# Linear attention and ELU feed-forward on one core: 1/P in PSUM, a late check of alpha, and a new issue order

## The chip, the cores and the metric

The kernel runs on one core of a Trainium2 chip. The metric is the device time of one execution in microseconds (us). TensorE is called PE, VectorE DVE, ScalarE ACT, GpSimd POOL and SyncE SP; SP issues nearly all DMAs.

## The reference

```python
B, H, S, D = 4, 8, 768, 48          # attention; then 3072 tokens, d_model 384, d_ff 2048
for t in range(S):
    state = alpha[:, :, t, :, None] * state + np.einsum('bhd,bhe->bhde', k[:, :, t], v[:, :, t])
    y[:, :, t] = np.einsum('bhd,bhde->bhe', q[:, :, t], state)
x = np.ascontiguousarray(y.transpose(0, 2, 1, 3)).reshape(B * S, H * D)
h = x @ w_in
g = np.where(h > 0.0, h, np.exp(np.minimum(h, 0.0)) - 1.0)
out = g @ w_out                      # everything in float32
```

## The kernel before

The attention works in 24 windows of 128 time steps (6 to a batch element), the feed-forward in 12 blocks of 256 tokens (two windows each), with d_ff cut into 8 slices j. Everything is a list of tokens of the form NAME.i: a function NAME is called with the index i and issues one or a few instructions. The list START (L49 to L76) is written out by hand and covers windows 0 to 11 in part and blocks 0 to 3; the list STEADY (L79), from block 4 on, repeats and is not touched. The tokens are issued in exactly this order, so that it sets the order on each engine's queue and on SP's DMA queue. Each engine takes its own instructions strictly in order.

A window i passes through these tokens. L (or LA for alpha and LB for k and q) loads k, q and alpha (`qka`, 770 KB, three buffers); LV loads v (four buffers, which hold the state too). SC (DVE, L202) is the running product P of alpha. LN and EX (ACT, L211, L216) make R = 1/P by a logarithm and an exponential; EX also adds up R into `chk_p`. KA (L224), KB (L229) and KC (DVE, L234) turn k into k/P with one Newton step, on DVE for the windows in KAV and KBV and on POOL for the others. PC (ACT, L238) adds up P into `chk_p`, as a check of alpha's range. SQ (L251, L254) is q times P, on DVE for the windows in SQV, else on POOL. TP (PE, L275) and KN (ACT, L305), or TA and TB (DVE, L285), transpose k. S (PE, L340, L324) and MK (DVE, L357, L352) are the masked scores, U (PE, L387, L369) is k times v, and UP, UA, UB, UC (L413, L404, L406, L435, L437) bring the state forward. YL, Y3 and Y (PE and ACT, L448, L453, L481, L493) make the output of the window, XH, XP, XL and XD split it into a high and a low float32r part.

Weights come in sixteen packed loads F.f (768 KB each; f = 2j for w_in, 2j+1 for w_out). Two of them make a pair p: KW (ACT, L572), DA (DVE, L586) and DB (DVE, L591) unpack a pair, WH (ACT, L618) rounds to the high part, WL (L638, on DVE for the f in WLV, else on POOL) subtracts to the low part. F.13 and F.15 land in a buffer (`spare`) that is read until WL.9 and WL.11 are done. LC, CA and CB check the packed weights later, through the one buffer with the tag `ck`. The feed-forward of block b and slice j is A (PE, 18 matmuls, L654) into a PSUM tile h, RA, RB (ACT), RC (DVE), GH (ACT) and GL (DVE, or POOL for the pairs in GQS; L662 to L693) for the ELU and its split into two parts, and O (PE, 12 matmuls, L707) into two PSUM tiles per block, which stay until Z.b copies them out.

All PSUM tiles come from one pool, `psa`, with 8 banks: a PE token that needs a new tile waits until the last reader of an old one has finished. X and the WARM loop (L126) are fillers, matmuls of 512 columns on constants whose result nobody reads.

Of the kernel before, what the change touches and what calls it, by code (L numbers as in the profile page):

```python
# [973 lines left out]
```

## Time and profile before

| what | value |
|---|---|
| timed runs | 473.01, 475.49, 475.50 us (median 475.49) |
| the profiled execution: its time, and the span of its instructions | 474.23 us, 472.5 us |
| PE busy | 461.9 us (98%) |
| DVE busy | 369.4 us (78%) |
| ACT busy | 313.8 us (66%) |
| POOL busy | 130.6 us (28%) |
| bytes moved by DMA | 61.13 MB, a mean of 129 GB/s |

The page gives busy time for each engine over the span. An engine that waits inside a group of matmuls can still look busy, so the share alone does not say what bounds a stretch; for that one reads the waits (who waited for whom), the timeline of one engine, and the chain of work that ended last. PE is busy in all of the span's 40 slices at 80% or more, apart from the last, and the DMA engines are full in the first five slices and below half after them.

### The profile page before, as it was taken

How to read it: one execution, taken by the hardware profiler on the slowest of the kernel's cores; microseconds unless marked ns; L12 is line 12 of the kernel's file. 1: busy time of each engine (PE TensorE's matmuls, PEld its weight loads, DVE VectorE, ACT ScalarE, POOL GpSimd, SP SyncE). 2: the span in 40 equal slices, each digit the busy share in tenths (PEclk: the TensorE clock that was granted, in tenths of full speed). 3: DMA queues.
4: the chain of work that ended last, by engine and by line, in shares of the span. 5: the costliest groups of instructions: out<-in, count | busy, mean ns of one | idle time of the engine just before them, and what ended most of it. 6: DMA issues, size and time to landing. Idle time of an engine off the chain costs nothing.

```text
span 472.5 us, 13139 instructions
## 1 busy us (share of the span) xinstructions
PE 461.9 (98%) x5413; PEld 446.1 (94%) x5414; DVE 369.4 (78%) x764; ACT 313.8 (66%) x664; POOL 130.6 (28%) x113
## 2 busy tenths in 40 slices
...
GB/s 308 400 411 416 140 1 181 54 104 151 73 115 101 35 173 168 148 73 177 139 72 153 164 68 152 164 72 153 154 84 151 81 88 52 68 44 10 2 35 40
DMA packets 20483, 61.13 MB, mean 129 GB/s; under 512 B 2880, under 2 KB 7872, under 8 KB 20416
## 3 DMA queue, kind: packets, MB, share of 16 engines
...
## 4 chain that ended last, share of the span: by engine, by line
PE 86%; DVE 6%; ACT 3%; DMA 3%; issue 1%; SPq 0%; DVEq 0%; ACTq 0%
PE h L654 37%; PE o L707 36%; PE y L453 4%; PE q L369 2%; PE q L324 2%; DMA raw<-in_wgt_dram 2%; PE wp L126 2%; DVE spare L591 1%; PE y L448 1%; DVE raw L586 1%; DMA qka<-in_qka_dram 1%; DVE w L638 1%; PE sc L340 1%; ACT w L618 1%; PE tp L275 1%
## 5 line engine op out<-in xcount | busy, mean ns | idle before, releaser
L654 PE MATMUL h<-xt,w 128*128 128x256 f32 x1728 | 202.3, 276 | 3.9 <-DVE gl L693 1.5
L654 PEld LDWEIGHTS h<-xt,w 128*128 128x128 f32 x1728 | 197.9, 192 | 5.3 <-DVE gl L693 1.7
L707 PE MATMUL o<-w,gh 128*128 128x384 f32 x768 | 189.0, 328 | 0.0
L707 PEld LDWEIGHTS o<-w,gh 128*128 128x128 f32 x768 | 132.4, 189 | 0.9
L707 PE MATMUL o<-w,gl 128*128 128x384 f32 x384 | 125.4, 327 | 0.0
L662 ACT ACTIVATE r<-h 128x512 f32<-128x512 f32 x96 | 56.5, 599 | 56.6 <-PE h L654 55.2
L285 DVE STREAM_TRANSPOSE kn<-qka 32x128 f32<-32x128 f32 x256 | 77.4, 302 | 4.0
L673 DVE SCALAR_TENSOR_TENSOR h<-r,h 128x512 f32<-128x512 f32 x79 | 53.7, 691 | 25.4 <-ACT r L667 25.0
L707 PEld LDWEIGHTS o<-w,gl 128*128 128x128 f32 x384 | 72.6, 189 | 0.2 <-DVE gl L693 0.2
L693 DVE TENSOR_TENSOR gl<-h,gh 128x512 fp32r<-128x512 f32 x79 | 54.0, 689 | 23.7 <-ACT gh L679 20.7
L679 ACT CAST gh<-h 128x512 fp32r<-128x512 f32 x79 | 46.0, 582 | 34.3 <-DVE h L673 23.4
L224 POOL TENSOR_TENSOR qka<-qka,R 128x512 f32<-128x512 f32 x19 | 25.8, 1360 | 144.1 <-ACT R L216 96.0
L667 ACT ACTIVATE r<-r 128x512 f32<-128x512 f32 x96 | 60.7, 634 | 1.7
L254 POOL TENSOR_TENSOR st<-qka,P 64x512 f32<-64x512 f32 x32 | 40.0, 1249 | 23.1 <-DVE P L202 9.6
L352 DVE TENSOR_TENSOR st<-q,mask 64x256 f32<-64x256 f32 x72 | 30.3, 421 | 8.3 <-PE q L324 7.1
L693 POOL TENSOR_TENSOR gl<-r,gh 128x512 fp32r<-128x512 f32 x17 | 23.7, 1397 | 42.3 <-ACT gh L679 27.9
L202 DVE TENSOR_TENSOR_SCAN P<-qka,first 128x516 f32<-128x516 f32 x24 | 30.8, 1286 | 4.5 <-ACT R L238 2.6
L211 ACT ACTIVATE R<-P 128x512 f32<-128x512 f32 x24 | 15.0, 631 | 28.4 <-DVE P L202 28.3
L604 ACT ACTIVATE ck<-ck,lim 128x384 int32<-128x384 int8 x32 | 23.8, 744 | 3.5 <-DMA ck<-in_wgt_dram 3.5
L609 ACT ACTIVATE ck<-ck,lim 128x384 f32<-128x384 int32 x32 | 23.0, 719 | 0.8
L453 PEld LDWEIGHTS y<-st,vs 128*64 128x64 f32 x576 | 17.7, 138 | 2.4 <-issue 2.3
L229 POOL TENSOR_TENSOR R<-P,R 128x512 f32<-128x512 f32 x16 | 19.0, 1190 | 1.2
...
## 6 DMA issues: line engine op xcount, KB each, us to landing
...
```

The source lines that it names most:

```text
L202: nc.vector.tensor_tensor_scan(out=P.rearrange("p n w -> p (n w)"), data0=t[:, 2 * NP * W:], data1=first.rearrange("p n w -> p (n w)"), in ...
L254: eng(SQV, i).tensor_tensor(out=st[r, a], in0=d["q"][r], in1=pw(i)[r], op=ALU.mult)
L285: nc.vector.transpose(out=kn[32 * t:32 * t + 32, :, 32 * g:32 * g + 32], in_=d["kt"][32 * g:32 * g + 32, :, 32 * t:32 * t + 32])
L352: nc.vector.tensor_tensor(out=d["st"][r, a, :, c * C:(c + 1) * C], in0=d["s4"][a][o], in1=mask[o].unsqueeze(1).broadcast_to([64, NP, C]), ...
L453: nc.tensor.matmul(out[64 * a:64 * a + m], lhsT=lhs(i, c, a)[:, n * D:n * D + m], rhs=d["st"][:, a, n, c * C:(c + 1) * C], start=start, st ...
L654: nc.tensor.matmul(h[:, f, :], lhsT=t[:, wi, ws], rhs=x[:, :, c, xi].rearrange("p a x -> p x a"), start=(f == 0 and k == 0), stop=(k == 8) ...
L662: nc.scalar.activation(out=r, in_=d["h"], func=AF.Relu, scale=-1.0)
L667: nc.scalar.activation(out=d["r"], in_=d["r"], func=AF.Exp, scale=-1.0)
L673: nc.vector.scalar_tensor_tensor(out=d["g"], in0=d["r"], scalar=-1.0, in1=d["h"], op0=ALU.add, op1=ALU.max)
L679: nc.scalar.copy(out=gh, in_=d["g"])
L693: q.tensor_tensor(out=gl, in0=d["g"], in1=d["gh"].bitcast(F32), op=ALU.subtract)
L707: nc.tensor.matmul(o[:, 0:DM], lhsT=gt[:, f, ms], rhs=t[:, wi, f * DM:f * DM + DM].rearrange("p (a x) -> p x a", a=2), start=(j == 0 and f ...
```

## The change

Window by window, R of windows 0 to 4 (RPS) is now a tile of the PSUM pool; POOL can't read PSUM, so KA and KB of these windows are all on DVE, and the lists KAV, KBV, SQV and WLV change. The sum over P of windows 0 to 5 (ALATE; PC) is gone. In its place LP loads alpha of that window a second time, into the buffer with the tag `ck`, and AC (ACT) makes one pass over it, relu(2^100 (alpha - 1.25)), with its sum into the same place of `chk_p`. WARM is 20, not 25. The matmuls of YL and Y of windows 0 to 5 go in another order: the two halves a of the partitions now alternate. START has the same tokens otherwise, in a new order; X.2.0 no longer stands first, and X.2.2 has gone ahead of TP.0. The diff, cut (of START the first lines of both; two more tuples, WHV and KNV, are empty and choose nothing):

```diff
 EARLY = 6
-WARM = 25
+WARM = 20
 
 
 QU, QS = 2, 6
 
 PAIRS = 10
 
-WLV, KAV, KBV, SQV = (0, 2, 4, 5, 8, 9, 11, 14), (0, 1, 2, 6, 9), (0, 1, 2, 3, 4, 6, 8, 9), (0, 1, 3, 4, 6, 11)
-
-
+WLV, KAV, KBV, SQV = (1, 4, 7, 8, 9, 10, 11, 12, 14), (0, 1, 2, 3, 4, 7), (0, 1, 2, 3, 4, 6, 11), (0, 2, 5, 11)
+
+
+WHV, KNV = (), ()
+RPS, ALATE = (0, 1, 2, 3, 4), (0, 1, 2, 3, 4, 5)
 WPE, XPE, GPE, UPE = (), (0, 1, 2), (), (1,)
...
 START = """
-X.2.0 LA.0 SC.0 LN.0 LB.0 LA.1 SQ.0 EX.0 KA.0 SC.1 KB.0 LB.1 LV.1 LN.1 LV.0 KC.0 TP.0 EX.1 KA.1 KB.1 KC.1 S.0 L.2 SQ.1
-KN.0 F.0 U.0 UC.0 PC.0 TP.1 KN.1 SC.2 LN.2 S.1 MK.1 MK.0 U.1 F.2 SQ.2 EX.2 KA.2 UA.0 L.3 UP.1 UC.1 KB.2 PC.1 YL.0 Y3.0
-DA.0 X.2.2 Y.0 KC.2 TP.2 LV.2 UA.1 YL.1 F.4 SC.3 S.2 KW.0 DB.0 F.6 XH.0 KN.2 LV.4 Y3.1 U.2 UA.2 Y.1 F.1 LN.3 EX.3 MK.2
-YL.2 UB.2 WH.2 WL.2 KA.3 KB.3 XH.1 F.3 Y3.2 F.5 SQ.3 XP.0 XL.0 WH.0 WL.0 XP.1 XL.1 KW.2 KW.1 Y.2 XH.2 DA.2 KC.3 A.0.1
-DB.2 WH.4 TP.3 KN.3 DA.1 WL.4 DB.1 A.0.0 RA.0.0 RB.0.0 LV.3 WH.6 RA.0.1 F.14 WL.6 S.3 U.3 WH.1 A.0.2 WL.1 UC.2 XP.2
-XL.2 MK.3 RA.0.2 UA.3 YL.3 RB.0.1 RC.0.0 F.7 GH.0.0 Y3.3 RB.0.2 WH.3 A.0.3 DA.3 F.8 KW.3 F.10 GL.0.0 WL.3 DA.4 RC.0.1
-Y.3 XH.3 L.4 RC.0.2 UB.3 O.0.0 RA.0.3 GH.0.1 GH.0.2 PC.2 XL.3 DB.3 A.1.3 L.6 A.1.0 F.12 GL.0.2 F.9 KW.4 WH.5 A.1.1
-WH.7 SC.4 LN.4 WL.5 GL.0.1 DB.4 RB.0.3 EX.4 O.0.1 DA.6 A.1.2 WH.10 WL.10 SQ.4 KA.4 LC.2 RA.1.0 RC.0.3 RA.1.3 RB.1.0
-GH.0.3 RC.1.0 F.11 GL.0.3 LV.5 RA.1.1 RB.1.1 DA.5 RB.1.3 RC.1.1 GH.1.0 KW.5 A.1.5 RC.1.3 UC.3 RA.1.5 GL.1.0 WL.7 KB.4
-O.0.2 O.0.3 PC.3 L.5 SC.5 RA.1.2 RB.1.2 GH.1.3 GL.1.3 WH.8 WL.8 RB.1.5 RC.1.5 GH.1.1 RC.1.2 O.1.0 LN.5 KW.6 A.0.4
-RA.0.4 DB.5 LV.7 WH.11 EX.5 RB.0.4 SQ.5 GH.1.2 KC.4 PC.4 DB.6 GL.1.1 RC.0.4 O.1.1 TP.4 KN.4 A.1.4 RA.1.4 GL.1.2 WH.14
-U.4 UA.4 UB.4 RB.1.4 KA.5 KB.5 KC.5 PC.5 RC.1.4 S.4 O.1.2 A.0.5 WH.9 WL.14 UC.4 WL.11 TP.5 KN.5 L.7 GH.0.4 O.1.3 WH.12
-RA.0.5 RB.0.5 WL.9 SC.7 SC.6 GH.1.4 GL.1.4 LN.7 A.1.7 F.13 GL.0.4 WL.12 O.0.4 MK.4 LN.6 RC.0.5 EX.6 U.5 KA.6 Y.4 CA.2
-CB.2 F.15 DA.7 UA.5 SQ.6 RA.1.7 S.5 GH.0.5 GL.0.5 EX.7 LV.6 A.0.6 RB.1.7 MK.5 KW.7 KB.6 KC.6 PC.6 RA.0.6 RB.0.6 A.1.6
-DB.7 O.1.4 GH.1.5 GL.1.5 XH.4 XL.4 RA.1.6 RC.1.7 O.0.5 RC.0.6 RB.1.6 RC.1.6 GH.1.6 TP.6 O.1.5 GL.1.6 S.6 KN.6 WH.13
-KA.7 KB.7 MK.6 Y.5 XH.5 XD.4 WL.13 XL.5 L.9 KC.7 TB.7 WH.15 U.6 GH.1.7 O.1.6 ZV.6 XD.5 WL.15 GH.0.6 GL.0.6 PC.7 L.8
-GL.1.7 SQ.7 A.0.7 RA.0.7 UA.6 UB.6 UC.6 RB.0.7 A.2.1 RA.2.1 O.0.6 RB.2.1 SC.8 LN.8 LC.1 EX.8 KA.8 RC.2.1 GH.2.1 O.1.7
...
+LA.0 LB.0 LA.1 SC.0 LN.0 X.2.2 EX.0 LB.1 L.2 SQ.0 X.2.0 SC.1 LN.1 EX.1 SQ.1 KA.0 KB.0 KC.0 TP.0 KA.1 KB.1 KC.1 LV.0
+KN.0 S.0 LP.3 AC.3 F.0 LV.1 U.0 MK.0 UA.0 F.2 UC.0 TP.1 KN.1 YL.0 Y3.0 SC.2 LN.2 EX.2 LV.2 L.3 F.4 S.1 Y.0 MK.1 XH.0
+SQ.2 KA.2 KB.2 KC.2 DA.0 U.1 UP.1 KW.0 TP.2 KN.2 S.2 UA.1 F.6 U.2 YL.1 UC.1 MK.2 Y3.1 XP.0 UA.2 YL.2 Y3.2 SC.3 LV.3
+DB.0 F.7 Y.1 LN.3 EX.3 KA.3 SQ.3 KB.3 F.5 XL.0 XH.1 WH.2 WL.2 KC.3 WH.0 Y.2 XH.2 LV.5 WL.0 XP.1 XL.1 TP.3 XP.2 S.3
+KN.3 UB.2 U.3 KW.2 DA.2 XL.2 LV.6 MK.3 UC.2 UA.3 A.0.1 KW.3 DB.2 DA.3 WH.4 YL.3 Y3.3 L.4 SC.4 RA.0.1 RB.0.1 A.0.0
+RA.0.0 Y.3 F.1 WH.6 RB.0.0 WL.4 WL.6 XH.3 LN.4 F.3 DB.3 XL.3 EX.4 RC.0.0 A.0.2 RA.0.2 RB.0.2 KA.4 A.1.1 RC.0.1 GH.0.1
+A.1.2 WH.5 F.8 DA.1 RC.0.2 KW.1 L.5 KB.4 KC.4 DB.1 A.0.3 GL.0.1 TP.4 WH.7 GH.0.2 A.1.0 GL.0.2 LP.5 UB.3 RA.1.1 UC.3
+GH.0.0 F.9 KN.4 WH.1 WH.3 GL.0.0 F.10 WL.1 SQ.4 S.4 MK.4 LV.4 U.4 RA.1.0 WL.5 RB.1.0 UA.4 RC.1.0 O.0.0 WL.3 KW.4 SC.5
+DA.4 DB.4 AC.5 A.1.3 RA.1.2 O.0.1 GH.1.0 UB.4 RB.1.2 RB.1.1 RC.1.1 WH.10 RA.0.3 RB.0.3 O.0.2 F.11 L.6 UC.4 GH.1.1
+GL.1.1 WL.10 WH.8 KW.5 RC.0.3 GH.0.3 A.1.5 GL.1.0 RC.1.2 O.1.0 O.1.1 RA.1.5 WL.7 RA.1.3 RB.1.3 GH.1.2 WL.8 DA.5 GL.0.3
+F.14 LN.5 EX.5 F.12 SC.6 DB.5 RB.1.5 LN.6 KA.5 EX.6 A.1.4 RA.1.4 RB.1.4 RC.1.5 O.0.3 L.7 RC.1.3 GH.1.3 WH.11 RC.1.4
+GH.1.4 WH.9 KW.6 A.0.4 RA.0.4 RB.0.4 GL.1.3 GL.1.2 O.1.2 O.1.3 SQ.5 KA.6 KB.6 GH.1.5 KB.5 A.0.5 KC.5 TP.5 GL.1.4 LP.4
+AC.4 RA.0.5 RB.0.5 KC.6 SC.7 TP.6 KN.5 WL.11 RC.0.4 GH.0.4 GL.0.4 WL.9 O.1.4 KN.6 F.15 DA.6 U.6 LN.7 UA.6 Y.4 RC.0.5
+U.5 DB.6 GL.1.5 UB.6 UC.6 LV.7 WH.14 F.13 S.5 L.8 WL.14 A.1.7 UA.5 WH.12 WL.12 KW.7 DA.7 MK.5 A.1.6 RA.1.7 SQ.7 RB.1.7
+RC.1.7 O.1.5 SQ.6 EX.7 RA.1.6 GH.0.5 RB.1.6 RC.1.6 GH.1.6 KA.7 LC.3 A.0.7 XH.4 XL.4 RA.0.7 RB.0.7 RC.0.7 PC.6 O.0.4
+GL.1.6 KB.7 Y.5 XH.5 S.6 DB.7 WH.13 WH.15 A.0.6 GL.0.5 O.0.5 GH.1.7 XD.4 XL.5 KC.7 TB.7 SC.8 WL.13 XD.5 CA.3 CB.3 PC.7
...
     chk_y = const.tile([128, 2, NWIN], F32, name="chk_y")
     nc.vector.memset(chk_y[:, 1, 0:DIRECT], 0.0)
-    lim = const.tile([128, 2], F32, name="lim")
+    lim = const.tile([128, 3], F32, name="lim")
+    nc.vector.memset(lim[:, 2:3], -1.25 * 2.0 ** 100)
     nc.vector.memset(lim[:, 0:1], 0.5625)
     nc.vector.memset(lim[:, 1:2], -9.0)
     win = [{} for _ in range(NWIN)]
+    ck = {}
     TOK = dict(X=X)
...
     @tok
     def LN(i):
-        R = win[i]["R"] = work.tile([128, NP, W], F32, name="R", tag="R")
+        if i in RPS:
+            R = psa.tile([128, NP, W], F32, name="rp", tag="pa")
+        else:
+            R = work.tile([128, NP, W], F32, name="R", tag="R")
+        win[i]["R"] = R
         nc.scalar.activation(out=R, in_=pw(i), func=AF.Ln)
     @tok
...
     @tok
     def PC(i):
         nc.scalar.activation(out=win[i]["R"], in_=pw(i), func=AF.Copy, accum_out=chk_p[:, 1, i:i + 1])
+
+    @tok
+    def LP(i):
+        t = ck["p", i] = work.tile([128, DM, 2], F32, name="cp", tag="ck", bufs=1)
+        nc.sync.dma_start(out=t.rearrange("p k two -> p (k two)")[:, 0:NP * AW], in_=qka[i, :, 2 * NP * W:QW])
+
+    @tok
+    def AC(i):
+        t = ck.pop(("p", i)).rearrange("p k two -> p (k two)")[:, 0:NP * AW]
+        nc.scalar.activation(out=t, in_=t, func=AF.Relu, scale=2.0 ** 100, bias=lim[:, 2:3],
+                             accum_out=chk_p[:, 1, i:i + 1])
     @tok
     def SQ(i):
...
...
     xt = {}
-    def ymm(i, out, n, c, a, m, start):
-        d = win[i]
-        if i < EARLY:
-
-            for s, r in ((0, slice(64 * a, 64 * a + D)), (1, slice(64 * a, 64 * a + 64))):
-                if s or i % NW or c:
-                    nc.tensor.matmul(out[64 * a:64 * a + m], lhsT=lhs(i, c, s)[r, n * D:n * D + m],
-                                     rhs=d["st"][r, s, n, c * C:(c + 1) * C], start=start, stop=True,
-                                     skip_group_check=True)
-                    start = False
+    def ymm(i, out, n, c, m, start):
+        d = win[i]
+        if i >= EARLY:
+            for a in range(2):
+                nc.tensor.matmul(out[64 * a:64 * a + m], lhsT=lhs(i, c, a)[:, n * D:n * D + m],
+                                 rhs=d["st"][:, a, n, c * C:(c + 1) * C],
+                                 start=start, stop=True, skip_group_check=True)
             return
-        nc.tensor.matmul(out[64 * a:64 * a + m], lhsT=lhs(i, c, a)[:, n * D:n * D + m],
-                         rhs=d["st"][:, a, n, c * C:(c + 1) * C],
-                         start=start, stop=True, skip_group_check=True)
+
+        for s in range(0 if i % NW or c else 1, 2):
+            for a in range(2):
+                r = slice(64 * a, 64 * a + (64 if s else D))
+                nc.tensor.matmul(out[64 * a:64 * a + m], lhsT=lhs(i, c, s)[r, n * D:n * D + m],
+                                 rhs=d["st"][r, s, n, c * C:(c + 1) * C], start=start, stop=True,
+                                 skip_group_check=True)
+            start = False
     def xs(i):
         blk, half = divmod(i, 2)
...
             return
         yl = d["yl"] = psa.tile([128, W], F32, name="yl", tag="pa")
         for c in range(2):
-            for a in range(2):
-                ymm(i, yl[:, c * C:(c + 1) * C], NP - 1, c, a, 64, c == 0)
+            ymm(i, yl[:, c * C:(c + 1) * C], NP - 1, c, 64, c == 0)
     @tok
     def Y3(i):
...
                                      start=(n == 0), stop=True, skip_group_check=True)
         for c in range(2):
             for n in range(nn):
-                for a in range(2):
-                    ymm(i, y[:, n, c * C:(c + 1) * C], n, c, a, D if direct else 64,
-                        not direct and c == 0 and n == 0)
+                ymm(i, y[:, n, c * C:(c + 1) * C], n, c, D if direct else 64, not direct and c == 0 and n == 0)
     @tok
     def XH(i):
...
```

## Rows read from the trace of the kernel before

**Rows 1.** The page's busy table: engine, us, share of the span, instructions
```profile
PE 461.9 (98%) x5413; PEld 446.1 (94%) x5414; DVE 369.4 (78%) x764; ACT 313.8 (66%) x664; POOL 130.6 (28%) x113
```

**Rows 2.** Busy time by stretch: length, engines with instructions, clock, DMA share, GB/s
```profile
40.00:50.00 10.00, 10.00 (x125) 9.80 (x124) 9.32 (x11) 9.83 (x16) 4.57 (x2) 1.00 1.02 412
...
165.00:440.00 275.00, 275.00 (x3207) 270.44 (x3206) 225.34 (x526) 185.45 (x416) 65.19 (x56) 1.00 0.36 112
```

**Rows 3.** Waits of PE: engine, tile, line, what ended them; total us, times, longest
```profile
PE h L654 <- DVE gl L693: 1.5, 1, 1.5
PE h L654 <- DVE vs L435: 1.0, 1, 1.0
PE h L654 <- DVE vs L406: 1.0, 1, 1.0
PE h L654 <- DVE kn L285: 0.3, 1, 0.3
PE q L369 <- ACT kn L305: 0.3, 1, 0.3
```

**Rows 4.** Timeline of PE, 2 to 11 us: start, duration, instruction, shape, count
```profile
2.08 8.11 PE L126 MATMUL wp<-first 128*128 128x512 bf16 x25 [2.08 <-DVE first L120]
10.03 0.59 PE L126 MATMUL xf<-first 128*128 128x512 bf16 x2
10.46 0.60 PE L275 MATMUL tp<-ident,qka 128*128 128x128 f32 x4
```

**Rows 5.** Timeline of DVE: GL.0.3, then WL.14, then WL.11 and WL.9
```profile
55.64 0.69 DVE L693 TENSOR_TENSOR gl<-h,gh 128x512 fp32r<-128x512 f32 x1
...
74.09 0.95 DVE L638 TENSOR_TENSOR w<-wm,w 128x768 fp32r<-128x768 f32 x1
...
75.23 1.82 DVE L638 TENSOR_TENSOR w<-spare,w 128x768 fp32r<-128x768 f32 x2
```

**Rows 6.** The chain that ended last: start us, us, what; weights F.13 and F.15
```profile
77.49 8.20 DMA raw<-in_wgt_dram
```

**Rows 7.** The same chain: S.2 and Y.3 on PE
```profile
21.23 0.88 PE sc L340 x31
...
41.32 1.40 PE y L448 x48
```

**Rows 8.** Timeline of DVE, 6 to 10 us: KA.0 and KC.0
```profile
6.40 0.69 DVE L224 TENSOR_TENSOR qka<-qka,R 128x512 f32<-128x512 f32 x1 [0.58 <-ACT R L216]
...
8.85 0.69 DVE L234 SCALAR_TENSOR_TENSOR qka<-R,qka 128x512 f32<-128x512 f32 x1
```

**Rows 9.** Timelines of POOL (WL.10, KA.4) and DVE (SQ.4, two RC), 51 to 56 us
```profile
51.91 1.92 POOL L638 TENSOR_TENSOR w<-spare,w 128x768 fp32r<-128x768 f32 x1 [4.75 <-DMA vs<-in_vv_dram]
53.79 1.72 POOL L224 TENSOR_TENSOR qka<-qka,R 128x512 f32<-128x512 f32 x1
...
52.08 2.30 DVE L251 TENSOR_TENSOR st<-qka,P 128x512 f32<-128x512 f32 x1
54.30 1.28 DVE L673 SCALAR_TENSOR_TENSOR h<-r,h 128x512 f32<-128x512 f32 x2
```

**Rows 10.** PE timeline (A.1.4, A.1.7), then the chain (A.0.6 with A.1.6, two O)
```profile
68.80 2.25 PE L654 MATMUL h<-xt,w 128*128 128x256 f32 x18
...
79.44 2.17 PE L654 MATMUL h<-xt,w 128*128 128x256 f32 x18
...
88.00 4.26 PE h L654 x36
92.25 3.90 PE o L707 x24
```

**Rows 11.** DVE's groups, 0 to 77 us: count, busy us, mean ns (DA, SC, UC)
```profile
L586 DVE TENSOR_SCALAR raw<-raw 128x1536 int32<-128x1536 int32 x7 | 8.9, 1267 | 0.0
L202 DVE TENSOR_TENSOR_SCAN P<-qka,first 128x516 f32<-128x516 f32 x6 | 7.9, 1318 | 1.0 <-DMA qka<-in_qka_dram 0.9
...
L435 DVE TENSOR_TENSOR vs<-q,P 128x192 f32<-128x192 f32 x3 | 1.1, 363 | 0.0
```

31 lines of the change are left out of this document (19 added, 12 removed).

## Prediction

> **What bounds the kernel now.** I read the busy table first [rows 1]: TensorE (PE) is busy 461.9 of 472.5 us, VectorE (DVE) 78%, ScalarE (ACT) 66%. A busy PE need not be a full one, so the stretches came next: from 165 to 440 us PE is busy for all 275.00 us, while from 40 to 50 us DVE and ACT are nearly full too (9.32 and 9.83 of 10) and the DMA engines move 412 GB/s [rows 2]. So the late two thirds are PE work end to end, nothing in them is touched by the diff, and the sum can only be made in the hand-ordered START part: its PE instructions, and the gaps between them. PE's own waits are five there besides the first one: 1.5, 1.0, 1.0, 0.3 and 0.3 us, 4.1 in all [rows 3]. The other thing on PE that computes nothing is the fillers, 25 from 2.08 us and two more from 10.03 us, up to the first real instruction at 10.46 us, TP.0 [rows 4].
>
> The three long waits are all for a PSUM bank (pool `psa`, 8 banks), and each ended with a reader of another tile: A.0.2 with UC.2 (L435), A.1.5 with GL.0.3 (L693), A.0.6 with UA.5 (L406) [rows 3]. UC.2 even stands behind A.0.2 in START. Behind these readers stood DVE: GL.0.3 ended at 56.33 us after DVE passes without a gap; UA.5 stood behind DA.7, which waited for a weight load from 77.49 to 85.69 us [rows 5, 6].
>
> **The change, part by part.** Durations are of the profiled execution: span 472.5 us, 474.23 us with what lies around it. The three timed runs are 473.01, 475.49 and 475.50; the four have a mean of 474.56, and I put the difference on that, as one execution is no better than another.
>
> *Fillers.* Two fillers of X.2.0 take 10.46 - 10.03 = 0.43 us, so 0.216 us each (512 columns, the 2.4 GHz level). The 25 take 7.95 us, which is about 12 at twice that (1.2 GHz) and 13 at 0.216 [rows 4]. The change puts 20 + 2 + 2 = 24 ahead of TP.0 in place of 27: those removed are of the fast kind, 3 x 0.216 = 0.65 us, and TP.0 can start at 9.81. X.2.2 leaves the place between YL.0 and Y.0 (another 0.43 us), where it covered the wait for Y3.0; S.1 (32 matmuls, about 0.9 us by 31 of S.2 in 0.88 us [rows 7]) now stands there and is longer. Total -1.1 us. The cover: TP.0 needs KC.0, which ended at 8.85 + 0.69 = 9.54 us; before KA.0 DVE idled 0.58 us for ACT [rows 8], and the new order puts SC.1 into that gap, so KC.0 ends some 0.5 us earlier, about 9.0. If SC.1's alpha lands late, KA.0 behind it on DVE waits too; ends 0 and +0.3 us, I take 0. Of the clock the rows show that PE ran at the low level for its first 5 us and then at the high one. The page "TensorE: Matmul & The Clock Gate" of the Trainium skill (part 1) says that the moment of the rise differs between runs; with all fillers at the low level three fewer would save 1.3 us in place of 0.65. No run here shows that.
>
> *1/P in PSUM, and KA/KB of windows 3 and 4 on DVE.* An operand in PSUM does not make a DVE pass shorter: KC.0, all in SBUF, took 0.69 us, and two RC passes that read h from PSUM took 1.28 together [rows 8, 9]. What it changes is the neighbourhood of GpSimd (POOL). SQ.4 on DVE, with two SBUF inputs, took 2.30 us beside POOL's WL.10, against the 0.69 of such passes alone; the RC pair, beside POOL's KA.4, was not stretched [rows 9]. So KA and KB of windows 0 to 4 can't be stretched any more, SQ.4 goes to POOL (-1.6 us of stretch on DVE), and KA.4 (1.72 us on POOL [rows 9]) becomes 0.6 us on DVE. The price is a bank from LN to KC.
>
> *PC to LP and AC.* Six ACT passes become six of the same length; three of them (0, 1, 2) move from the full stretch to behind 95 us. Each AC waits on ACT's queue for its own load, with KN, LN and RA behind it: AC.3 is the only one close to its load, and KN.1 behind it has to wait for TP.1 anyway, which stands behind S.0 and U.0. Each LP is 128 x 516 words, 258 KB, 0.64 us at 412 GB/s [rows 2]; only LP.3 and LP.5 go on SP's queue while the DMA engines are full, so F, LV and L loads behind them come 0.64 to 1.3 us later. DVE waited for no weight load before 85 us, so I take 0; ends 0 and +0.6.
>
> *Matmuls of YL and Y.* Old order: 48 in 1.40 us, 29.2 ns each; S, which already alternates the halves, 31 in 0.88 us, 28.4 ns each [rows 7]. 384 matmuls x 0.8 ns: 0 to -0.3 us; I take 0.
>
> *The new order.* All five waits lose their cause as they stand: -4.1 us. What is late next? START's PE work is the same, so I put the time at which PE comes to a piece (old start, corrected for the pieces moved past it, old waits and the 1.1 us) against its last producer on DVE (old end, corrected in the same way). Prices: A 2.13 and O 1.95 us; S 1.0, Y 1.9, TP and U 0.5 (by the two rows of 32 and 48 small matmuls); on DVE 0.6 for a 512-column pass (two RC in 1.28), WL 0.91, SC 1.3, DA 1.27, a U step 0.3 [rows 5, 9, 10, 11].
> - A.1.4 waits for GL.0.3's bank. PE: 68.80 [rows 10] - O.0.3 - A.0.4 (4.1) + S.4 + U.4 (1.5) - 2.5 - 1.1 = 62.6. DVE: GL.0.3 at 56.33 [rows 5], less SQ.1, 3, 4, WL.0, 2, 5, DA.6 and the stretch (7.4), plus 19 pieces moved ahead of it (SQ.2, KA.3, KA.4, KB.4, KC.4, four U steps, WL.1, 7, 8, 10, MK.4, SC.5, RC.1.1, GL.1.0, RC.1.2, DA.5: 12.8): 61.7. Covered by 0.9.
> - A.1.7 waits for WL.14. PE: 79.44 + TP.6, O.1.4, U.6, Y.4, U.5, S.5 (6.4) - 2.8 - 1.1 = 81.9. DVE: WL.14 at 75.04, less 6.2 (the same without DA.6), plus 14.4 (KA.3, 4, SQ.2, 5, WL.1, 7, 9, 10, 11, MK.4, UC.4, SC.6, 7, KB.6, KC.6, GL.1.4, RC.0.5, UB.6, UC.6): 83.2, late by 1.3 if DVE waits as long as before, by nothing if it doesn't.
> - A.1.6, the second of the two from 88.00 us, started at 90.1 [rows 10]; with TP.6, O.1.4, U.6 (3.0) ahead of it and O.0.4, A.0.6 (4.1) not, it comes at 90.1 + 3.0 - 4.1 - 3.8 - 1.1 = 84.1, and may get the bank that MK.5 reads. MK.5 stands behind DA.7, DA.7 waits for F.15 and F.13, which SP sends after WL.9 has freed their buffer. WL.9 ended at 77.05; new order and less stretch leave it there (nine pieces and the stretch go, 10.2; thirteen come, 10.0), less what DVE no longer waits: 73 to 77. The load takes 8.6 us as before (77.05 to 85.69), DA.7 and MK.5 1.9: 83.5 to 87.5, so 0 to 3.4 us late.
>
> New waits thus lie between 0 and some 3.5 us; I take 1.5, the middle of the last one, since the first two are near their cover. Sum: -1.1 - 4.1 + 1.5 = -3.7 us, 470.5 on the profiled execution, **470.9** on the mean of the four.
>
> **Rivals.**
> *All cover holds* (A.1.6 gets another bank, UA.5's): -5.2 us, 469.4. For it: DVE waits less when PE is earlier. Against: the one order that the trace shows has three bank waits.
> *The banks cost as much as before.* Counting the tiles alive in START, the old order has 8 places at which seven banks are taken and the next tile must have the last one; the new has 13, for R stands in a bank and O.1's two follow O.0's sooner. The three bank waits, 3.5 us [rows 3], over 8 places are 0.44 us each, over 13 they are 5.7: 474.56 - 5.2 + 5.7 = 475.1. For it: the waits were of this kind. Against: at A.1.4, one of the 13, cover was found above. Beside it stands the page "PSUM — Partial Sum Buffer" of the Trainium skill (summary: rules for kernel authors), which tells authors to evacuate PSUM promptly as it is tight; keeping R there goes against it, and this rival is what it would do.
> *POOL collides with DVE* (slower). POOL takes WL.0, 2, 3, 5, 6 and SQ.1, 3, 4 ahead of WL.9, beside DVE's two-input DB and SC; each collision costs about the 1.6 us of SQ.4 [rows 9] and puts off WL.9, so the loads of F.15 and F.13, so DA.7, at which both ACT (KW.7) and DVE then stand. A lag of 5.2 + 2.4 us at A.1.6 means WL.9 at about 81.2, three collisions more than now; five more: 474.56 - 5.2 + (8.0 + 3.4) = 480.8. Against: the old order had as many POOL passes there.
> *R in PSUM does nothing*: DVE then keeps its lost time, and the case is that of the banks.
>
> **How the numbers follow.** Forecast 0.48 (469.5 to 472.8); all covered 0.17; banks 0.20; collisions 0.08; 0.07 for what no row shows. The range takes in the two neighbours, with 1.2 us of the runs' own spread below the lower: 468.2 to 475.3. About 0.5% (2.4 us) is what a measurement of this kernel can tell from no change: faster 0.66 (forecast, all covered and a little of the rest), the same 0.25 (banks, some rest), slower 0.09.
>
> **What would show it.** Right: TP.0 at 9.8 us, right behind the fillers; no wait before Y.0; PE's waits within START at 1 to 2 us, the longest near A.1.6 and ended by MK.5 or DA.7; DVE's passes on R at 0.69 us beside a busy POOL. Wrong: PE idle between the fillers and TP.0; new waits of 4 us and more ended by readers of h tiles (banks); DB or SC at 2.5 us and more beside WL on POOL; a wait for LP on ACT with PE behind it; more than 0.2 us of gaps behind 165 us.

## The result: 0.7% slower, where 3.7 us less were forecast

| | before | after |
|---|---|---|
| time, median of 20 runs each | 473.14 us | 477.20 us |
| ratio, 95% interval | | 1.0069 [1.0046, 1.0092] |
| profiled execution: time, span | 474.23, 472.5 us | 478.38, 476.7 us |
| last matmul of PE ends at | 468.44 us | 470.81 us |
| PE idle from its first filler to its last matmul | 4.5 us | 7.0 us |

The range of the forecast ended at 475.3. The medians are of all runs; the ratios here and below compare only runs in the chip's faster state, which leaves out 1 of the 20 of after, 1 of the 6 of tuned and 3 of the 12 of r_sbuf, its profiled one among them, whose idle time isn't given for that reason. In the two profiled executions PE ends 2.4 us later; the other 1.8 us of the span lie behind PE. There the last output takes 3.5 us to land in place of 1.9. It takes 3.8 in before_lpac_psum below, which has the old order, and 1.9 in l4_early, which has the new one, so I don't put that part down to the change.

The page's busy table of after (answers [rows 1]) shows PE as busy as before, in a longer span:

```profile
PE 461.8 (97%) x5409; PEld 446.5 (94%) x5409; DVE 371.3 (78%) x763; ACT 316.6 (66%) x664; POOL 135.1 (28%) x115
```

The waits of PE in after (engine, tile, line, what ended them; total us, times, longest; answers [rows 3]):

```profile
PE h L679 <- DVE w L663: 1.7, 1, 1.7
PE o L732 <- DVE w L663: 1.7, 1, 1.7
PE y L477 <- issue: 1.1, 1, 1.1
PE sc L363 <- DVE gl L718: 0.9, 1, 0.9
PE tp L294 <- POOL st L270: 0.5, 1, 0.5
PE h L679 <- ACT ck L631: 0.4, 1, 0.4
PE u L436 <- issue: 0.3, 1, 0.3
PE h L679 <- DVE vs L458: 0.2, 1, 0.2
```

Not one of the five waits of [rows 3] is left, as forecast. But eight others stand there, 6.8 us in all, and the two longest are not waits for a bank. They are for `w L663`, the low half of a weight (WL), which A.0.2 and O.0.0 read. The timeline of PE has them in their places (start us, duration, instruction, shape, count, idle time before):

```profile
39.20 8.47 PE L679 MATMUL h<-xt,w 128*128 128x256 f32 x70 [1.67 <-DVE w L663]
...
51.01 1.09 PE L363 MATMUL sc<-st,qka 48*64 48x64 f32 x30 [0.89 <-DVE gl L718]
...
54.64 0.43 PE L732 MATMUL o<-w,gh 128*128 128x384 f32 x1 [1.67 <-DVE w L663]
...
57.10 3.24 PE L679 MATMUL h<-xt,w 128*128 128x256 f32 x18
```

The last of these rows is slow for another reason: the same 18 matmuls take 2.17 us elsewhere. PE goes on at 54.64, after the pauses of 0.89 and 1.67 us, and from about 56 us the granted clock falls, to 0.50 of 2.4 GHz (1.2 GHz) up to 59 us and to 0.66 as a mean of these 5 us. It didn't fall behind A.0.2's pause, which was as long, 1.67 us, so the length of a pause alone doesn't decide it (busy time by stretch: length, PE with instructions, granted clock, DMA share, GB/s):

```profile
39.00:44.00 5.00, 4.67 (x39) 1.00 1.03 413
...
50.00:55.00 5.00, 2.44 (x69) 1.00 1.01 386
55.00:60.00 5.00, 5.00 (x28) 0.66 0.43 153
...
56.00:59.00 3.00, 3.00 (x14) 0.50 0.43 144
```

That is (1 - 0.66) x 5 = 1.7 us of matmuls lost, beside the waits themselves.

What DVE did ahead of the three pauses (its timeline: SC.4, WL.4, DB.1, GL.0.2, WL.1):

```profile
35.50 1.23 DVE L206 TENSOR_TENSOR_SCAN P<-qka,first 128x516 f32<-128x516 f32 x1 [1.59 <-DMA qka<-in_qka_dram]
36.65 2.50 DVE L663 TENSOR_TENSOR w<-spare,w 128x768 fp32r<-128x768 f32 x1
...
46.61 3.66 DVE L613 SCALAR_TENSOR_TENSOR spare<-raw 128x1536 int32<-128x1536 int32 x1 [0.35 <-ACT raw L594]
50.15 0.71 DVE L718 TENSOR_TENSOR gl<-h,gh 128x512 fp32r<-128x512 f32 x1
...
52.04 2.54 DVE L663 TENSOR_TENSOR w<-spare,w 128x768 fp32r<-128x768 f32 x1
```

And what POOL did at the same moments (WL.6, WL.5, WL.3):

```profile
36.38 1.95 POOL L663 TENSOR_TENSOR w<-spare,w 128x768 fp32r<-128x768 f32 x1 [5.95 <-ACT w L643]
...
46.59 1.83 POOL L663 TENSOR_TENSOR w<-wm,w 128x768 fp32r<-128x768 f32 x1
51.94 1.82 POOL L663 TENSOR_TENSOR w<-spare,w 128x768 fp32r<-128x768 f32 x1 [3.52 <-ACT w L643]
```

Lay the two side by side. POOL's WL.6 ends at 38.33; DVE's WL.4, which by its row began at 36.65, ends at 39.15, 0.82 us later, about as long as a WL takes alone (0.95 in [rows 5]). POOL's WL.5 ends at 48.42 and DVE's DB.1 at 50.27, 1.85 later, a DB's own time. POOL's WL.3 ends at 53.76 and DVE's WL.1 at 54.58, 0.82 later. Each time POOL began first, by 0.02 to 0.27 us, and the pass on DVE ends as if it had only begun when POOL had finished. The Trainium skill has a rule that says so, on the page "SBUF — State Buffer", section "SBUF: two separate sides": the two engines share one pair of ports, a DVE pass with two SBUF inputs needs it, and whoever comes second waits for the whole instruction of the other. The three pairs of rows agree with it to 0.13 us.

### The profile page after: what moved, and what is told of

It reads as the page before. It is cut to its first block, busy times and chain, and to the rows that moved or that the text cites. A ratio compares the mean times of both kernels' runs of the same rounds, so it can differ in the third digit from the quotient of the medians.

```text
span 476.7 us, 13154 instructions
## 1 busy us (share of the span) xinstructions
PE 461.8 (97%) x5409; PEld 446.5 (94%) x5409; DVE 371.3 (78%) x763; ACT 316.6 (66%) x664; POOL 135.1 (28%) x115
## 4 chain that ended last, share of the span: by engine, by line
PE 79%; DVE 6%; DMA 5%; ACT 4%; issue 2%; SPq 1%; POOL 1%; ACTq 0%; POOLq 0%; DVEq 0%
PE o L732 36%; PE h L679 34%; PE y L469 4%; DMA qka<-in_qka_dram 4%; PE q L347 2%; PE q L392 2%; DMA raw<-in_wgt_dram 1%; DVE w L663 1%; DVE spare L613 1%; DVE gl L718 1%; ACT w L643 1%; PE sc L363 1%; DVE h L698 1%; PE y L477 1%; ACT raw L594 1%
## 5 line engine op out<-in xcount | busy, mean ns | idle before, releaser
L232 POOL TENSOR_TENSOR qka<-qka,R 128x512 f32<-128x512 f32 x18 | 23.7, 1319 | 139.6 <-ACT R L224 89.1
L273 POOL TENSOR_TENSOR st<-qka,P 64x512 f32<-64x512 f32 x34 | 44.8, 1317 | 23.8 <-DVE P L206 9.7
L206 DVE TENSOR_TENSOR_SCAN P<-qka,first 128x516 f32<-128x516 f32 x24 | 29.6, 1233 | 5.7 <-DMA qka<-in_qka_dram 5.6
L219 ACT ACTIVATE R<-P 128x512 f32<-128x512 f32 x19 | 12.0, 629 | 25.4 <-DVE P L206 25.4
L631 ACT ACTIVATE ck<-ck,lim 128x384 f32<-128x384 int32 x32 | 22.9, 717 | 0.8
L237 POOL TENSOR_TENSOR R<-P,R 128x512 f32<-128x512 f32 x17 | 20.2, 1189 | 3.5 <-DVE qka L232 2.3
L469 PEld LDWEIGHTS y<-st,vs 128*64 128x64 f32 x576 | 17.8, 138 | 2.5 <-issue 2.5
```

The source lines that it names most:

```text
L206: nc.vector.tensor_tensor_scan(out=P.rearrange("p n w -> p (n w)"), data0=t[:, 2 * NP * W:], data1=first.rearrange("p n w -> p (n w)"), in ...
L273: eng(SQV, i).tensor_tensor(out=st[r, a], in0=d["q"][r], in1=pw(i)[r], op=ALU.mult)
L469: nc.tensor.matmul(out[64 * a:64 * a + m], lhsT=lhs(i, c, a)[:, n * D:n * D + m], rhs=d["st"][:, a, n, c * C:(c + 1) * C], start=start, st ...
```

## The experiments

Five theories were set against each other. **1**: DVE and POOL exclude each other where DVE reads SBUF alone, and that makes WL.4, DB.1 and WL.1 late. **2**: the late load L.4 holds DVE's queue at SC.4 (1.59 us above), and all else follows from it. **3**: the banks that R takes. **4**, for the wait `y <- issue`, which nothing in the trace releases: PE waits for its own code. And, as in the prediction, each part of the change was to have its own price. In the expectations the pass at 46.61 is called DB.4, and the one that S.4 waits for GL.0.0; by the order on DVE they are DB.1 and GL.0.2.

| kernel | median us | ratio to before, 95% interval | PE idle, us |
|---|---|---|---|
| changed kernel | 477.20 | 1.0069 [1.0046, 1.0092] | 7.0 |
| wl_apart | 474.33 | 1.0027 [0.9998, 1.0055] | 6.3 |
| l4_early | 476.73 | 1.0063 [1.0036, 1.0090] | 5.6 |
| both | 475.62 | 1.0049 [1.0022, 1.0076] | 6.8 |
| r_sbuf | 478.09 | 1.0083 [1.0051, 1.0116] | not given |
| tuned | 476.47 | 1.0079 [1.0050, 1.0107] | 5.6 |
| no_early_lp | 484.93 | 1.0269 [1.0248, 1.0290] | 11.6 |
| f57_late | 480.50 | 1.0141 [1.0110, 1.0172] | 8.0 |
| f4567_late | 480.66 | one run; before 471.66 | 9.5 |
| before_lpac | 485.76 | 1.0275 [1.0254, 1.0296] | 10.6 |
| before_lpac_psum | 489.70 | 1.0360 [1.0339, 1.0380] | 12.6 |
| before_warm20 | 472.63 | 0.9991 [0.9962, 1.0021] | 3.6 |
| before_sq4 | 472.92 | 0.9990 [0.9968, 1.0012] | 3.5 |
| before_best | 470.77 | 0.9937 [0.9913, 0.9962] | 0.8 |

### wl_apart: POOL's three passes put on DVE

```diff
-WLV = (1, 4, 7, 8, 9, 10, 11, 12, 14)
+WLV = (1, 3, 4, 5, 6, 7, 8, 9, 10, 11, 12, 14)
```

> The changed kernel with the low halves WL.3, WL.5 and WL.6 put on DVE instead of POOL; order and all else as changed. In the changed kernel's trace WL.4 (DVE 36.65, 2.50 us), DB.4 (46.61, 3.66 us) and WL.1 (52.04, 2.54 us) each end one lone duration (0.9, 1.8 and 0.9 us) after a pass of POOL that began earlier. Theory 1 (the two engines exclude each other): the three passes take 0.93 to 1.0 and 1.8 us again, the PE waits for A.0.2 (1.67), S.4 (0.89) and O.0.0 (1.67) fall to 0 to 0.5 each, PE doesn't pause long enough to drop to 1.2 GHz behind O.0.0 (2.2 us), while DVE has 3 passes of 0.95 more: 3.5 to 6 us under the changed kernel, 0.994 to 0.999 of before. Theory 2 (the load L.4 comes late and holds the DVE queue from SC.4 on): DVE is as late and has 2.9 us more to do, O.0.0's wait stays at 1.5 or more: 1.004 to 1.010. Theory 3 (banks: the tiles of R take PSUM): the waits stay, 1.007.

Timeline of DVE in wl_apart: WL.4 and WL.6, then DB.1, then WL.1:

```profile
37.16 1.80 DVE L663 TENSOR_TENSOR w<-spare,w 128x768 fp32r<-128x768 f32 x2
...
46.49 1.97 DVE L613 SCALAR_TENSOR_TENSOR spare<-raw 128x1536 int32<-128x1536 int32 x1 [0.41 <-ACT raw L594]
...
50.24 0.95 DVE L663 TENSOR_TENSOR w<-spare,w 128x768 fp32r<-128x768 f32 x1
```

The passes are back at 0.9 each, 1.97 and 0.95 us: theory 1 has the mechanism. O.0.0 and S.4 no longer wait, A.0.2 waits 0.49, and the clock stays at 2.4 GHz. The time falls by 1.0069 - 1.0027 = 0.42%, 2.0 us, where theory 1 had 3.5 to 6; the two intervals just overlap, so that even these 2.0 are not clear of noise. The waits of PE in wl_apart tell why it is so little:

```profile
PE h L679 <- DVE w L663: 1.3, 3, 0.6
PE y L477 <- issue: 1.2, 1, 1.2
PE h L679 <- ACT ck L631: 1.1, 1, 1.1
PE h L679 <- DVE xt L556: 1.0, 1, 1.0
PE tp L294 <- issue: 0.6, 1, 0.6
PE h L679 <- ACT w L643: 0.5, 1, 0.5
```

DVE now carries 2.9 us more, and PE, no longer held at 39 and 54, comes to the next pieces earlier: A.1.1 waits 1.04 us for XL.3, which stands behind DB.3 on DVE, A.1.5 waits 1.12 for WH.10 and WL.10, and A.2.0 1.10 (0.45 in after). So most of the gain is made and handed back. PE reaches O.0.1, right behind the stretch in question, at 55.51 us in wl_apart and at 60.18 in after, 4.7 earlier; A.2.0 starts at 104.76 and 106.20, 1.4 earlier; and PE ends 1.4 earlier (469.44 against 470.81). First wl_apart, then after:

```profile
55.51 0.49 PE L732 MATMUL o<-w,gh 128*128 128x384 f32 x2
...
104.76 2.25 PE L679 MATMUL h<-xt,w 128*128 128x256 f32 x18 [1.10 <-ACT ck L631]
```

```profile
60.18 0.49 PE L732 MATMUL o<-w,gh 128*128 128x384 f32 x2
...
106.20 2.25 PE L679 MATMUL h<-xt,w 128*128 128x256 f32 x18 [0.45 <-ACT ck L631]
```

That the three stretched passes caused these pauses is thus shown, and the fall of the clock went with them; that without them the kernel would be as fast as forecast is not, since other waits take their place.

### l4_early and both: the late load

```diff
-... XH.2 LV.5 WL.0 ... LV.6 ... YL.3 Y3.3 L.4 SC.4
+... XH.2 L.4 LV.5 WL.0 ... LV.6 ... YL.3 Y3.3 SC.4
```

> The changed kernel with the load L.4 ahead of LV.5 and LV.6 on SP's queue, which wait there for Y.1 and XP.2; all else as changed. The load can then be issued when S.1 has read its buffer, at about 14.5 us, not at 28.55. Theory 1 (DVE and POOL exclude each other): SC.4 no longer waits (1.59), starts at about 33.9, WL.4 is through before POOL's WL.6 starts, so A.0.2's wait of 1.67 goes; the later collisions DB.4 beside WL.5 and WL.1 beside WL.3 hang on their places and mostly stay: 0.5 to 2.5 us under the changed kernel, 1.002 to 1.006 of before. Theory 2 (the late load is the cause of all that follows): all three waits and the low clock go, 5 to 6 us less, 0.993 to 0.997. Theory 3 (banks): 1.007, no change.

> The changed kernel with both edits: L.4 ahead of LV.5, and WL.3, WL.5 and WL.6 on DVE. Theory 1: as with the low halves on DVE alone, or up to 1 us better, since SC.4's wait of 1.59 no longer stands in DVE's queue, which now carries 2.9 us more: 0.992 to 0.997 of before. Theory 2: 0.993 to 0.998. Theory 3 (banks): 1.007.

SC.4 no longer waits and WL.4 takes 0.98 us at 36.67, ahead of POOL's WL.6 (38.29); A.0.2's wait is gone. DB.1 (3.44 us) and WL.1 (2.54) are still stretched beside WL.5 and WL.3, O.0.0 still waits 1.67 and the clock still falls behind it. So L.4's lateness only decided whether WL.4 came behind WL.6, and theory 2 falls for the rest. (WL.6 on POOL now takes 2.72 us beside DVE's DB.3, in place of 1.83: POOL loses as well when it comes second.) Yet the time didn't fall by A.0.2's 1.67 either, only to 1.0063. Waits of PE in l4_early:

```profile
PE o L732 <- DVE w L663: 1.7, 1, 1.7
PE y L477 <- issue: 1.1, 1, 1.1
PE tp L294 <- POOL st L270: 1.0, 1, 1.0
PE sc L363 <- issue: 1.0, 1, 1.0
```

The fourth is new: S.3 pauses 0.95 us for nothing that the trace names, like Y.1. Both edits together (1.0049) show the same new pause, and are no better than wl_apart alone; theory 1 had 0.992 to 0.997 for them, so this too is a miss.

### f57_late and f4567_late: the pause that nothing releases

```diff
-F.7 Y.1 ... KB.3 F.5 ... XH.2 LV.5 WL.0            (on top of wl_apart)
+Y.1 ... KB.3 ... XH.2 LV.5 F.7 F.5 WL.0            f57_late
+Y.1 ... KB.3 ... XH.2 LV.5 F.4 F.6 F.7 F.5 WL.0    f4567_late, F.4 and F.6 from 11.4 us
```

> wl_apart with the weight loads F.7 and F.5 (1.5 MB, issued at 13.2 us) behind LV.5 on SP's queue (25.3 us). In each trace of the new order PE pauses 1.05 to 1.23 us in Y.1, waiting for nothing that the profile names, at its 705th instruction, 256 behind the pause in UP.1 (449th), and goes on 1.4 to 1.6 us after a 16 KB packet of the instruction queue. Theory 4 (PE waits for its own code, whose packet queues behind 8 MB of loads): with 1.5 MB less in front the packet comes earlier and the pause falls to 0 to 0.4, while KW.3 and DA.3 wait for their raw words to about 33 and SC.4, WL.4 follow 1 to 2 us later: 1.001 to 1.007 of before in all. If the pause is something else, it stays at 1.05 to 1.23.

> wl_apart with four weight loads (F.4, F.6, F.7, F.5: 3.1 MB, issued at 11.4 to 14.5 us) behind LV.5 on SP's queue (25.3 us): one look at the pause of PE in Y.1 alone, the rest of the start is knowingly late (KW.2 and all that follows by 6 to 10 us). With f57_late the stretch of full transfers ended at 22.7 us, a microsecond after the 16 KB packet at 21.69, and the pause stayed at 1.05. Here it ends at about 16 to 18 us. Theory 4 (the packet of PE's code queues behind the loads): the packet of the second 256 instructions comes 1 to 2 us after PE passes the 449th instruction instead of 3.8 and the pause at the 705th is 0 to 0.3. If the fetch has a fixed time of its own: the packet comes 3 to 4 us after and the pause stays at 0.9 to 1.2.

Counted as matmuls and weight loads, PE's pauses of this kind stand at its 449th (UP.1), 705th (Y.1) and 961st (S.3, only in l4_early and both) instruction: 256 apart. Three kernels of the old order show the second one too (0.42 us in before_warm20, 0.77 in before_sq4, 0.24 in before_lpac). In every case PE goes on 1.35 to 1.6 us after a packet of the instruction queue (16 KB each by the profile's page: 44 packets, 0.72 MB) has ended. In after that packet ran from 21.51 to 22.54 us. Timeline of PE in after, Y.1:

```profile
22.42 0.50 PE L477 MATMUL y<-st,vs 48*48 48x64 f32 x10
23.98 1.23 PE L477 MATMUL y<-st,vs 48*48 48x64 f32 x37 [1.05 <-issue]
```

With F.7 and F.5 away the packet still came at 21.69, in a stretch still at full rate (the transfers ebbed at 22.7), and the pause stayed at 1.05, where theory 4 had 0 to 0.4: a miss. With four loads away the queues were empty when it was due. The packet ran from 19.07 to 20.25, 1.1 us after PE's 449th instruction (3.8 in after), and Y.1 went through. Stretches 16 to 22 us of f4567_late (PE, granted clock, DMA share, GB/s), then Y.1 on PE:

```profile
16.00:18.00 2.00, 1.66 (x36) 1.00 0.99 399
18.00:20.00 2.00, 2.00 (x41) 1.00 0.50 193
20.00:22.00 2.00, 2.00 (x75) 1.00 0.01 5
```

```profile
22.61 1.53 PE L477 MATMUL y<-st,vs 48*48 48x64 f32 x48
```

So theory 4 holds as far as one execution of f4567_late shows it: PE waited for its code, whose packet came late while the queues were full of loads. The time of these two kernels is of no interest, since KW.2 and KW.3 wait for their weights (a wait of PE of 2.6 and of 2.5 and 3.8 us for YL and Y).

### r_sbuf, before_lpac and before_lpac_psum: the banks of R

```diff
-RPS = (0, 1, 2, 3, 4)
+RPS = ()                                            r_sbuf, from the changed kernel
-PC.0 ... PC.5                                       before_lpac, from the kernel before:
+LP.i AC.i, i = 0 to 5, between CB.2 and RB.0.7      R still in SBUF, KA.3 and KA.4 on DVE
+R = psa.tile(...) for windows 0 to 4                before_lpac_psum, on top of it
```

> The changed kernel with R of spans 0 to 4 in SBUF again (order, lists of engines, fillers and loads as changed). Theory 3 (R's five tiles take PSUM that h, sc and o then wait for, 0.44 us at each of 13 tight places against 8): S.4's wait of 0.89 on GL.0.0 and about 1 to 2 us more go: 0.999 to 1.005 of before. Theory 1 (DVE and POOL exclude each other where DVE reads SBUF alone): nothing of the three long passes changes, and KA, KB of spans 3 and 4 now read SBUF alone and wait for POOL too where they meet it: 0 to 1.5 us over the changed kernel, 1.007 to 1.010.

> The kernel before with one part of the change: the sum over P (PC) of spans 0 to 5 gone, and the second load with its check (LP, AC) in its place, all six between 85 and 105 us; KA of spans 3 and 4 on DVE, so that it can be compared with before_lpac_psum. R stays in SBUF, fillers, order and all else as before. The prediction takes 0 (0 to +0.6): 0.999 to 1.002 of before. If ACT's work of 0.92 each and the loads meet F.15 and the windows' loads there: 1.002 to 1.006.

> before_lpac with R of spans 0 to 4 in PSUM: the step of the change that puts R into a bank, in the old order. Theory banks (the rival at 0.44 us for each tight place): five tiles more among eight, in an order not made for them, +2 to +5 us over before_lpac: 1.004 to 1.011 of before. Theory 1 (DVE and POOL exclude each other only where DVE reads SBUF alone): KA and KB of the five spans no longer wait for POOL, in the old order few of them meet it: -1 to +0.5 us against before_lpac.

In the new order, giving the banks back gains nothing on balance (1.0083 against 1.0069, intervals overlapping). In its profile O.0.0 still waits 1.66 us and S.4 1.10, so R's banks are not the cause of these waits, and theory 3 falls for them. What the banks alone cost there stays open, for the run changes a second thing: with R in SBUF, KA.3, KB.3 and KC.3 are stretched beside POOL's SQ.3, WL.2 and WL.0, to 1.68, 2.22 and 2.17 us from 0.68, 0.69 and 0.69. KA.3 and KB.3 on DVE in r_sbuf:

```profile
27.77 1.68 DVE L232 TENSOR_TENSOR qka<-qka,R 128x512 f32<-128x512 f32 x1
29.49 2.22 DVE L237 TENSOR_TENSOR R<-P,R 128x512 f32<-128x512 f32 x1
```

In the old order putting R into PSUM costs 1.0360 - 1.0275 = 0.85%, 4 us. Timeline of PE in before_lpac, the wait for GL.0.3:

```profile
54.87 1.38 PE L667 MATMUL h<-xt,w 128*128 128x256 f32 x10 [0.44 <-DVE gl L706]
```

and in before_lpac_psum:

```profile
54.92 1.27 PE L671 MATMUL h<-xt,w 128*128 128x256 f32 x9 [2.58 <-DVE gl L710]
```

GL.0.3 is done at the same time in both (its rows end at 54.82 and 54.86), and PE goes on at the same time. But with R.4 in a bank it has to stop one group of 18 matmuls (2.17 us) sooner. That is what a bank costs, where an order wasn't made for one bank less. PE's idle time grows by 2.0 us between the two (10.6 to 12.6); the other half of the 4 us is open.

The absolute time of before_lpac is a failure of mine, and a lesson on the moved step. I put LP.0 behind CB.2, on whose buffer it waits, and ahead of the load F.15 on SP's queue: A.0.6 waits 4.5 us for UA.5 behind F.15's DA.7, and another group 4.0 us for a transfer of `xt` that SP sends late. Both replaced nothing but waits of 0 to 1 us in before.

### no_early_lp: the second loads

```diff
-LB.1 ... LP.3 AC.3 F.0 ... LP.5 ... AC.5 ... LP.4 AC.4   (in the early part)
+LP.0 AC.0 LP.3 AC.3 ... LP.4 AC.4 LP.2 ... LP.1 KC.9 AC.1 LP.5 AC.5
```

> The changed kernel with the second loads and checks of alpha of spans 3, 4 and 5 moved to 105 to 130 us, behind those of spans 0, 2 and 1; nothing else changed. LP.3 (258 KB) is issued at 3.68 us in the changed kernel, ahead of F.0; LP.5 at 32.4, LP.4 at 55.2. The prediction's price for an early second load is 0.64 us for every load behind it: L.4 lands 0.6 earlier and SC.4's wait of 1.59 becomes 1.0; if DVE's lateness from SC.4 on is what costs, the time falls 0.3 to 0.8 us: 1.004 to 1.007 of before. If code fetches in the crowded queues cost (PE's waits that nothing releases, 0.35 and 1.05), they shrink as well: 1.002 to 1.006. If ACT's late checks now stand before what PE waits for: 1.007 to 1.010.

Early, little changes (the pause of Y.1 stays at 1.22, A.0.2's wait goes, as in l4_early). Late, it costs 1.0269 - 1.0069 = 2.0%, some ten microseconds. The wait of ACT for these loads in no_early_lp, and then in after:

```profile
ACT cp L256 <- DMA cp<-in_qka_dram: 9.1, 3, 3.5
```

```profile
ACT cp L256 <- DMA cp<-in_qka_dram: 0.8, 1, 0.8
```

All LP share one buffer. Where two pairs follow each other, SP can send the second load only when AC has read the first, and AC of the second, next on ACT's queue, waits for the whole transfer: AC.0 has read at about 111.2 us, and AC.3 starts at 114.22, after 2.93 us of waiting. PE's next pieces stand behind it (a U's wait of 2.9 us for its KN among them). In after a pair stands alone, and its AC waits 0.8 us at most. PE's idle time grows by 4.6 us, and the clock falls twice; I didn't account for the rest. None of my three expectations had this size: where an LP and its AC stand was worth more than any other edit to the new order.

### before_warm20, before_sq4 and before_best: the same lessons on the kernel before

```diff
-WARM = 25
+WARM = 20                                           before_warm20, before_best
-SQV = (0, 1, 3, 4, 6, 11)
+SQV = (0, 1, 3, 6, 11)                              before_sq4, before_best
-DA.1 WL.4 DB.1 ... WL.1 UC.2    F.15 DA.7 UA.5
+DA.1 WL.4 UC.2 DB.1 ... WL.1    F.15 UA.5 DA.7      before_best alone
```

> The kernel before with 20 fillers in place of 25, nothing else: one part of the change alone. The prediction prices five fillers at 0.216 us each, of which TP.0 can use what KC.0 (done at 9.5) leaves: -0.65 to -0.95 us with what follows on DVE and ACT at the same places: 0.998 to 0.9987 of before. If DVE's and ACT's first passes set TP.0 or what stands behind it (the stream of small matmuls, KN.0, KC.1): 0.999 to 1.000. If the lighter start lets the clock rise later: 1.000 to 1.002.

> The kernel before with SQ.4 on POOL instead of DVE, nothing else. In before's trace SQ.4 takes 2.30 us on DVE (52.08) beside WL.10 on POOL (51.91, 1.92 us), and A.1.5 on PE waits 1.5 us for GL.0.3 four passes behind it. Theory 1 (DVE and POOL exclude each other where DVE reads SBUF alone): with SQ.4 off DVE the pass RC.0.3 starts at 52.2 instead of 54.3, GL.0.3 ends near 54.2, A.1.5's wait falls to 0 to 0.2: 0.9965 to 0.998 of before. If POOL, now 1.2 us longer, keeps KA.4 or WL.7 back so that another pass on DVE is locked instead: 0.999 to 1.001.

> The kernel before with four small edits, each at a wait of PE that its trace shows: 20 fillers; SQ.4 on POOL (A.1.5's wait of 1.5); UC.2 ahead of DB.1 on DVE (A.0.2's wait of 1.0); UA.5 ahead of DA.7 on DVE, which waits 2.1 there for the load F.15 (A.0.6's wait of 1.0). If waits that are taken away are not given back elsewhere: -3 to -4.5 us, 0.9905 to 0.994 of before. If half comes back under other names, as it did in the changed kernel: 0.994 to 0.998.

SQ.4 was the stretched pass of [rows 9]. Off DVE, RC.0.3 starts at 52.00 instead of 54.30, GL.0.3 ends at 54.62 instead of 56.33, and A.1.5's wait of 1.5 us [rows 3] is gone. Each single edit ends PE 1.1 to 1.4 us earlier in its profile, which its time can't yet tell from no change. All four together can: 0.9937, 3.0 us less than before. Waits of PE in before_best, besides the first one:

```profile
PE h L654 <- DVE kn L285: 0.3, 1, 0.3
PE q L369 <- ACT kn L305: 0.3, 1, 0.3
```

This is faster than both kernels, with R in SBUF, the sum over P and the old order kept.

### tuned: the same treatment of the new order

```diff
+XL.3 ahead of DB.3; SC.5 behind WL.10; DB.7 WH.13 WH.15 behind XL.5   (on top of wl_apart)
```

> The changed kernel with WL.3, WL.5 and WL.6 on DVE (as in wl_apart) and four moves on DVE's queue (one takes two passes of ACT along): XL.3 ahead of DB.3, SC.5 behind WL.10, and DB.7 (with WH.13 and WH.15) behind XL.5. Each is drawn from a PE wait that wl_apart's trace still shows: 1.04 for XL.3 behind DB.3, 0.54 and 0.58 for WH.10 and WL.10 behind SC.5, 1.10 at 103.67 for what I read as XL.5 and its transfer behind DB.7. If PE's time in this stretch is set by the order of DVE's queue (theory 1), 2 to 3.2 us go: 470.5 to 472.5, 0.994 to 0.998 of before. If something else is next in line at each place (banks, loads, instruction fetch), the waits come back under another name: 1.001 to 1.004.

This missed. A.1.1's and A.2.0's waits went, but A.2.4, one group on, now waits 1.43 us for MK.6's bank, A.1.5 still 0.54, and two others 0.24 and 0.66. PE's idle time fell by 0.7 us, and the time is not better than wl_apart's. By the ratios it is 0.5% slower than wl_apart, with intervals that just overlap, though its profiled execution is shorter (475.42 against 477.30); why is open.

## Why the prediction was wrong

*Fillers: right in size, as far as single profiles show it.* TP.0 starts at 9.25 us, 1.2 earlier than in [rows 4]; before_warm20, with this part alone, ends PE 1.1 us earlier (467.30 against 468.44), and its time can't be told from no change. But it is not "right behind the fillers", one of the signs I had named for wrong. Timeline of PE in after:

```profile
7.70 1.03 PE L128 MATMUL xf<-first 128*128 128x512 bf16 x4
9.25 0.63 PE L294 MATMUL tp<-ident,qka 128*128 128x128 f32 x4 [0.52 <-POOL st L270]
```

The fillers were through at 8.72, KC.0 at 9.15 (forecast 9.0), and the row names POOL's SQ.1 (done at 9.09), which TP.0 doesn't read. KC.0 on DVE:

```profile
8.46 0.69 DVE L242 SCALAR_TENSOR_TENSOR qka<-rp,qka 128x512 f32<-128x512 f32 x1
```

So KC.0, not the fillers, set the start. In the kernels of the new order the same 24 fillers end between 8.7 and 9.9 us. The Trainium skill's page "TensorE: Matmul & The Clock Gate" (part 1), cited in the prediction, has the moment of the clock's rise differ between runs, and these ends agree. But only in `both` did the fillers end behind KC.0 and hold TP.0; in the others the start follows KC.0 by 0.1 us.

*R in PSUM: right.* KA.3 and KB.3 take 0.68 and 0.69 us beside a busy POOL, and 1.68 and 2.22 with R in SBUF. What I left out is that POOL was to get passes in their place which meet DVE's others.

*PC to LP and AC: right that nothing waits for AC, wrong on the loads.* I reasoned that DVE had waited for no weight load before 85 us. It was not a weight load that came late but an alpha load: L.4 is issued at 28.55 us, behind LV.5 (which SP holds 9.2 us for Y.1) and LV.6, and SC.4 waits 1.59 us for it. I had priced the loads behind an LP, but not those that the new order moves behind other waits on SP's queue. By itself this cost little (l4_early).

*Matmul order of YL and Y: right.* The 368 matmuls in the trace take 12.8 us as before (12.9).

*The new order: the step that failed.* All five old waits went, -4.1 us. The new ones were to be 1.5 us, with 3.5 as the worst; they are 6.8, and the low clock takes 1.7 more. I had tested three places (A.1.4, A.1.7, A.1.6) because they wait for the banks that the old waits were for, and at those three PE indeed doesn't wait. (The list of pieces for A.1.7 adds up to 13.5 us at its own prices, not 14.4, so that it was late by 0.4 and not 1.3; the forecast doesn't hang on it.) But nothing in the sum asked when WL.4 and WL.1 are ready for A.0.2 and O.0.0, which read them. The three pauses behind stretched passes are 4.2 us (1.67 + 0.89 + 1.67), the clock 1.7, the two code pauses 1.4 (0.35 + 1.05), TP.0 0.5.

In sum: PE was to end at 468.44 - 3.7 = 464.7 and ends at 470.8. Of these 6.1 us, 5.1 are waits (7.0 against 4.5 - 4.1 + 1.5 = 1.9) and 1.7 the clock; the fillers, 1.0 better than forecast in this execution (their busy time falls by 2.1), take 1.0 back, and 0.3 is left over. The new order's waits are the term that was mis-sized; the low clock is a term that the sum didn't have.

*The rivals.* "POOL collides with DVE" had the mechanism and the size of one collision (1.6 us; WL.4 and WL.1 lost 1.6, DB.1 1.8), but I placed it at WL.9, F.15 and DA.7, and gave it 0.08 with the argument that the old order had as many POOL passes there. That argument is the mistake. What counts is not the number of POOL's passes but which DVE pass they meet: in before a collision on the path was one of SQ.4, worth 1.5 us; in after they met WL.4, DB.1 and WL.1, on which PE waits directly. The banks, at 0.20, explain S.4's 0.89 only as a follow-up (it goes when DB.1 is no longer stretched).
